# Narrow transposes and remainder products widened to the full 128x128 array, in an attention and convolution block with its gradients

## The chip, the cores and the metric

The kernel runs on one core of a Trainium2 chip. Its time is the device time of one execution in microseconds. Engines are named as in the profile: PE is TensorE (the 128x128 array), PEld its weight loads, DVE is VectorE, ACT is ScalarE, POOL is GpSimd, and SP is the sync engine, which issues nearly all DMAs here.

## The reference

One block of an E-Branchformer and its gradients, in bf16, for 2 batches of T = 4000 tokens and D = 144 channels. The results are the output and the gradients of x and of the seven weights.

```python
def _fwd_reference(x, w_qkv, w_att_out, w_mlp_in, dw_csgu, w_mlp_out, dw_merge, w_merge):
    xa = _layernorm(x)
    q, k, v = split(einsum('btd,de->bte', xa, w_qkv), 3)
    p = softmax(einsum('btd,bsd->bts', q, k) * D ** (-0.5))
    glob = einsum('btd,de->bte', einsum('bts,bsd->btd', p, v), w_att_out)
    u, g = split(gelu(einsum('btd,de->bte', xa, w_mlp_in)), 2)
    gc = depthwise_conv5(_layernorm(g), dw_csgu)          # over time, 5 taps
    loc = einsum('btd,de->bte', u * gc, w_mlp_out)
    m = concatenate([glob, loc])
    m = m + depthwise_conv5(m, dw_merge)
    return x + einsum('btc,cd->btd', m, w_merge)

_out, _vjp = jax.vjp(_f, x, w_qkv, w_att_out, w_mlp_in, dw_csgu, w_mlp_out, dw_merge, w_merge)
_grads = _vjp(grad_out)
```

(The splits and the convolutions are written out in the original; `depthwise_conv5` and `split` stand here for slices and a loop over the taps.)

## The kernel before

Tokens lie in blocks of 128 on the partitions: 32 blocks (NBK) a batch, in 8 groups (NGR) of four. A row of 144 channels doesn't fit 128 partitions once it is transposed. So every transposed tensor has a main part (channels 0 to 127) and a remainder of 16 channels (DR = 16), and much of the code deals with remainders: they are put together from several tensors (`t3`: 32 + 16 = 48 columns; `g80` and the tap arrays: 5 x 16 = 80).

`bounded` runs three stages for each batch, and one at the end.

- `phase_head` norms x, transposes it and makes the arrays Q and B that the attention needs.
- `phase_attn` goes through 32 rows of blocks (`unit`, `xfill`, `yz`), forward and backward in one pass. Products with QBr (L1768) use 16 rows of the array, four of them side by side. In between, `Steps` places pieces of the local branch (`pair`, `tapcorr`), a fixed order written out with `manual_schedule`. A pair of blocks calls `Chan.put` twice (once for the normed gate `gn`, once for its gradient `dgc`): four transposes into one PSUM tile (L1476 and L1478), two ACT copies, and a DMA that stores the remainder five times, shifted by one token each (`Taps.store`). `Taps.load` brings 80 rows back for the convolution. SP issues these DMAs in order with the transposing DMAs of P and S (L1786).
- `phase_tail` goes through 16 pairs of blocks in rounds h, two rounds to a group g. `turn` transposes Y (h = 0) and ug (h = 1) of a group, and stores their remainders as taps. `corr` adds up EF (L1944), the correlations behind some weight gradients. `turn_dx` transposes four parts of two blocks (L1954), `parts(i)`, the last of which is `t3`; `turn_dx2` copies them from PSUM to hT, and `dx_mm` multiplies hT by W.WIM (L1987). `out_mm` (L1969, L1970) makes the output of the pair four rounds earlier. In four last rounds `gr_part` (L2038) multiplies the same four parts by xaa, eight blocks a call, for further weight gradients. `prep`, on POOL, fills `t3` and `g80` of the next group.
- `finish_weights` makes the weight gradients from EF and gr.

A transpose on PE has the data as stationary operand, so the array's columns in use are the width of the slice that is transposed: 128, 16 or 48 here. A round of the tail stands in this order (cut):

```python
                if hf == 0 and g < NGR:
                    turn(g, 0); corr(g, 0); turn(g, 1); corr(g, 1)
                elif g < NGR:
                    corr(g, 2); corr(g, 3)
                if h < NPR:
                    tt = turn_dx(h)
                    turn_dx2(*tt)
                ...
                if 0 <= h - 4 < NPR:
                    out_mm(h - 4)
                ...
                if h < NPR:
                    dx_mm(h)
                if hf == 1 and g + 1 < NGR:
                    prep(g + 1)
```

W.WIM[:, 3, :] is set to zero before its first 48 rows are filled, in the kernel before as well.

Of the kernel before, what the change touches and what calls it, by code (L numbers as in the profile page):

```python
# [7 lines left out]
BF = mybir.dt.bfloat16  # L8
# [6 lines left out]
D = 144  # L15
DR = 16
# [1042 lines left out]
NBK = 32  # L1059
# [401 lines left out]
class Chan:  # L1461
# [8 lines left out]
    def put(self, p, src):  # L1470
        nc = self.k.nc
        t = self.t[p] = self.pool.tile([128, 260], BF, tag=self.name, bufs=3, name=self.name)
        r_ = self.pool.tile([128, 256], BF, tag=self.name + "s", bufs=2, name=self.name + "s")
        pm = self.ps.tile([128, 4, 128], BF, tag="f", name="pm")
        for j in range(2):
            nc.tensor.transpose(pm[:, j, :], src[:, j, 0:128], self.W.ident[:])  # L1476
        for j in range(2):
            nc.tensor.transpose(pm[0:DR, 2 + j, :], src[:, j, 128:D], self.W.ident[:])  # L1478
        nc.scalar.copy(r_[0:DR, :], pm[0:DR, 2:4, :].rearrange("p a b -> p (a b)"))
        nc.scalar.copy(t[:, 2:258], pm[:, 0:2, :].rearrange("p a b -> p (a b)"))  # L1480
        self.taps.store(r_[0:DR, :], p * 256, 256)
        if p == 0:
            nc.gpsimd.memset(t[:, 0:2], 0.0)
        else:
            u = self.t[p - 1]
            nc.gpsimd.tensor_scalar(t[:, 0:2], u[:, 256:258], 1.0, 0.0, op0=ALU.mult, op1=ALU.add)
            nc.gpsimd.tensor_scalar(u[:, 258:260], t[:, 2:4], 1.0, 0.0, op0=ALU.mult, op1=ALU.add)
        if p == NBK // 2 - 1:
            nc.gpsimd.memset(t[:, 258:260], 0.0)
# [389 lines left out]
def phase_tail(k, W, b, S):  # L1879


    nc, tc = k.nc, k.tc
    with ExitStack() as es:
        pp = es.enter_context(tc.tile_pool(name="tl_big", bufs=1))
# [8 lines left out]
        uT = main_arr(k, pp, "uT")  # L1893
        taps = [Taps(k, "y80_%d" % b), Taps(k, "u80_%d" % b)]
        dh = pp.tile([128, NBK, 2 * D], BF, name="dhr")
        t3 = pp.tile([128, NBK, 48], BF, name="t3r")
        EF = ps_e.tile([128, 4, 512], F32, tag="EF", name="EF")
        id_ = W.ident
        G, st = {}, {}
# [11 lines left out]

        def prep(g):
            r = slice(g * 4, g * 4 + 4)
            nc.gpsimd.tensor_scalar(t3[:, r, 0:32], dh[:, r, 256:2 * D], 1.0, 0.0, op0=ALU.mult, op1=ALU.add)
            nc.gpsimd.tensor_scalar(t3[:, r, 32:48], S.Zn[:, r, 128:D], 1.0, 0.0, op0=ALU.mult, op1=ALU.add)
            g80 = G["g80", g] = lx.tile([128, 4, 80], BF, tag="g80", name="g80")
            nc.gpsimd.tensor_scalar(g80[:].rearrange("p a (m r) -> p a m r", r=DR), G["gs", g][:, :, :, 128:D], 1.0, 0.0, op0=ALU.mult, op1=ALU.add)

        def turn(g, h):

            src = (S.Yn[:, g * 4:g * 4 + 4, :], G["ug", g])[h]
            pt = ps_t.tile([128, 8, 128], BF, tag="tp", name="pt")
            for j in range(4):
                nc.tensor.transpose(pt[:, j, :], src[:, j, 0:128], id_[:])
            for j in range(4):
                nc.tensor.transpose(pt[0:DR, 4 + j, :], src[:, j, 128:D], id_[:])
            nc.scalar.copy((yT, uT)[h][:, 2 + g * 512:2 + (g + 1) * 512], pt[:, 0:4, :].rearrange("p a b -> p (a b)"))
            r_ = wk.tile([128, 512], BF, tag="r16_%d" % h, name="r16")
            nc.vector.tensor_copy(r_[0:DR, :], pt[0:DR, 4:8, :].rearrange("p a b -> p (a b)"))
            taps[h].store(r_[0:DR, :], g * 512, 512)  # L1930

        def fill(g):
            for h in range(2):
# [11 lines left out]
                                     start=(i == 0 and q % 3 == 0), stop=(i == NBK - 1), skip_group_check=True)  # L1945

        def parts(i):
            return [(dh[:, i, 0:128], 128), (dh[:, i, 128:256], 128), (S.Zn[:, i, 0:128], 128), (t3[:, i, :], 48)]

        def turn_dx(p):  # L1950
            pt = ps_t.tile([128, 8, 128], BF, tag="tp", name="pt")
            for q in range(2):
                for n_, (p_, w) in enumerate(parts(2 * p + q)):
                    nc.tensor.transpose(pt[0:w, n_ * 2 + q, :], p_, id_[:])  # L1954
            hT = st["hT", p] = wk.tile([128, 8, 128], BF, tag="hT", bufs=2, name="hT")
            return pt, hT

        def turn_dx2(pt, hT):
            nc.scalar.copy(hT[:, 0:6, :], pt[:, 0:6, :])
            nc.scalar.copy(hT[0:48, 6:8, :], pt[0:48, 6:8, :])  # L1960

        def out_mm(p):
            g = p // 2
# [18 lines left out]
        def dx_mm(p):  # L1982
            hT = st.pop(("hT", p))
            po = ps_o.tile([128, 2, D], F32, tag="o", name="po")
            for q in range(2):
                for n_, (_, w) in enumerate(parts(0)):
                    nc.tensor.matmul(po[:, q, :], hT[0:w, n_ * 2 + q, :], W.WIM[0:w, n_, :], start=(n_ == 0), stop=(n_ == 3))  # L1987
            t = st["t", p] = wk.tile([128, 2, D], F32, tag="t", bufs=4, name="t")
            nc.vector.tensor_tensor(t[:], po[:], S.acc[:, 2 * p:2 * p + 2, :], op=ALU.add)
# [42 lines left out]
        def gr_part(r):  # L2032
            if r[0] == 0:
                st["gr"] = ps_e.tile([128, 4, 512], F32, tag="EF", name="gr")
            gr = st["gr"]
            for i in r:
                for n_, (p_, w) in enumerate(parts(i)):
                    nc.tensor.matmul(gr[0:w, n_ // 2, (n_ % 2) * D:(n_ % 2 + 1) * D], p_, S.xaa[:, i, :],  # L2038
                                     start=(i == 0 and n_ % 2 == 0), stop=(i == NBK - 1), skip_group_check=True)
# [11 lines left out]
        with tc.manual_schedule():  # L2051
            loads(0)
            load_x(0)
            loads(1)
            prep(0)
            for h in range(NPR + 4):
                g, hf = divmod(h, 2)
# [5 lines left out]
                if hf == 0 and g < NGR:  # L2063
                    turn(g, 0)
                    corr(g, 0)
                    turn(g, 1)
                    corr(g, 1)
                elif g < NGR:
                    corr(g, 2)
                    corr(g, 3)  # L2070
# [3 lines that stand above are left out]
# [15 lines left out]
                if hf == 1 and g + 1 < NGR:  # L2089
                    prep(g + 1)  # L2090
# [143 lines left out]
def bounded(k):  # L2234
    nc, tc = k.nc, k.tc
    with tc.tile_pool(name="n_w", bufs=1) as wp, tc.tile_pool(name="n_acc", bufs=1) as ap:
# [9 lines left out]
        for b in range(2):  # L2246
            with tc.tile_pool(name="n_res%d" % b, bufs=1) as res:
                S = W_()
                S.xaa = res.tile([128, NBK, D], BF, name="xaa")
                S.xaT = res.tile([128, NBK * 128], BF, name="xaT")  # L2250
                S.XR = res.tile([128, 4, 512], BF, name="XR")
                S.Q_t = res.tile([128, NBK, D], BF, name="Q_t")
                S.B_t = res.tile([128, NBK, D], BF, name="B_t")
                S.rstd_x = res.tile([128, NBK], F32, name="rstdx")
                S.ug_d = tc.dram_tile([128, NBK, D], BF, name="ug_d%d" % b)
                S.gn_d = tc.dram_tile([2 + NBK * 128 + 2, D], BF, name="gn_d%d" % b)
                nc.sync.dma_start(S.gn_d[0:2, :], k.zero[0:2, :])
                nc.sync.dma_start(S.gn_d[2 + NBK * 128:4 + NBK * 128, :], k.zero[0:2, :])
                S.dh_d = tc.dram_tile([128, NBK, 2 * D], BF, name="dh_d%d" % b)
                S.dug_d = tc.dram_tile([128, NBK, D], BF, name="dug_d%d" % b)  # L2260
                phase_head(k, W, b, S)
                with tc.tile_pool(name="n_att%d" % b, bufs=1) as at:
                    S.early = at
                    S.acc = at.tile([128, NBK, D], F32, name="acc2")
                    nc.gpsimd.memset(S.acc[:], 0.0)

                    S.Yn, S.Zn = S.Q_t, S.B_t
                    phase_attn(k, W, b, S)
                    phase_tail(k, W, b, S)
# [49 lines left out]
```

## Time and profile before

| | |
|---|---|
| median of 3 runs | 1528.79 us (1527.81 to 1530.97) |
| profiled execution | span 1533.1 us; no other time of it is given |
| granted PE clock, mean | 0.939 |
| PE busy | 1364.5 us, 89% of the span |
| DVE busy | 886.1 us, 58% |
| ACT busy | 820.7 us, 54% |
| POOL busy | 567.4 us, 37% |
| batch 0 | attention from about 80 to 624 us, tail to about 735 us |
| batch 1 | attention from about 800 to 1342 us, tail to about 1455 us |

In the profile, a form such as 128*48 128x144 on PE says that 128 rows and 48 columns of the array are used, then the partitions and elements of the operands. A duration on PE runs from the start of a product to its modelled end, and products overlap: what one costs is seen from the distance to the next one's start. The stretches of the span give busy time by engine; the chain of waits follows what ended last back from the end.

### The profile page before, as it was taken

The page shows a single profiled execution, that of the slowest core. Times are in us where ns is not written, and L with a number is a line of the kernel's source. Part 1 is how long each engine was busy: PE and PEld are TensorE (multiplying, and loading weights), DVE is VectorE, ACT ScalarE, POOL GpSimd, SP SyncE. Part 2 cuts the span into 40 slices and gives each one's busy share as a digit, 9 for nine tenths or more (in the row PEclk, how much of TensorE's full clock was granted, in tenths as well). Part 3 has the DMA queues.
Part 4 walks back from the last instruction along what each step waited for, and adds up shares of the span by engine and source line. Part 5 has one row for each costly group of instructions (what it writes and reads, how often), then busy time and mean ns, then how long its engine had stood idle before and what let it go on. Part 6 is the DMA issues. An engine that isn't in the chain of part 4 may idle for free. (4 is left out here: it accounts for less than half of the span.)

```text
span 1533.1 us, 40191 instructions
## 1 busy us (share of the span) xinstructions
PE 1364.5 (89%) x15366; PEld 990.8 (65%) x15366; DVE 886.1 (58%) x3021; ACT 820.7 (54%) x2473; POOL 567.4 (37%) x1049
## 2 busy tenths in 40 slices
PE   5989999999999999899779999999999999989932
PEld 3727767676776767687553767677667667868610
DVE  5545676676676666344335666676776676534332
ACT  4746656566656654343365666666656565444210
POOL 2233444444344433343232444344444442334200
PEclk9959999999999999999896999999999999999955
DMA  5348978898988799654525988998999988856320
GB/s 143 105 86 149 169 136 162 155 170 150 163 153 163 131 192 171 146 171 116 158 77 99 165 153 147 170 164 154 164 160 147 170 158 163 162 156 180 78 87 13
DMA packets 652289, 220.66 MB, mean 144 GB/s; under 512 B 589876, under 2 KB 649012, under 8 KB 652084
## 3 DMA queue, kind: packets, MB, share of 16 engines
q1 hardware_dynamic: 651220, 217.89, 73.0%
q8 instruction: 122, 2.00, 0.6%
q14 instruction: 83, 0.68, 0.2%
q10 hardware_dynamic: 864, 0.09, 0.0%
HBM read 58.00 MB, written 25.13 MB: 54 GB/s over the span
## 5 line engine op out<-in xcount | busy, mean ns | idle before, releaser
L1778 DVE SCALAR_TENSOR_TENSOR Sm<-pD,Pm 128x500 bf16<-128x500 f32 x512 | 331.2, 675 | 286.8 <-ACT Pm L1777 226.4
L1777 ACT ACTIVATE Pm<-pS 128x500 bf16<-128x500 f32 x512 | 294.9, 582 | 125.9 <-PE pS L1772 123.0
L1839 POOL TENSOR_TENSOR acc<-xs,acc 128x432 f32<-128x432 f32 x160 | 179.8, 1124 | 395.9 <-ACT xs L1838 393.9
L1834 PE MATMUL X<-Bt,Pm 128*128 128x144 bf16 x2048 | 293.6, 227 | 1.0 <-DVE Bt L1806 1.0
L1833 PE MATMUL X<-Qs,Sm 128*128 128x144 bf16 x2048 | 293.7, 227 | 0.5 <-POOL Qs L1797 0.5
L1833 PEld LDWEIGHTS <-Sm 128*128 128x128 bf16 x2048 | 201.5, 98 | 19.2 <-issue 2.6
L1834 PEld LDWEIGHTS <-Pm 128*128 128x128 bf16 x2048 | 201.2, 98 | 18.8 <-issue 2.1
L1772 PE MATMUL pS<-xaT,QTm 128*128 128x500 bf16 x512 | 162.0, 400 | 0.0
L1772 PE MATMUL pD<-xaT,BTm 128*128 128x500 bf16 x512 | 160.1, 396 | 0.0
L1838 ACT COPY xs<-X 128x432 f32<-128x432 f32 x160 | 83.2, 520 | 138.4 <-PE X L1834 137.4
L1816 PE MATMUL y<-xaa,PT 128*128 128x144 bf16 x2048 | 150.4, 227 | 1.2 <-DVE B_t L1824 1.2
L1768 PE MATMUL pD<-XR,QBr 16*128 16x500 bf16 x512 | 131.0, 392 | 21.1 <-DVE Sm L1778 19.6
L1816 PE MATMUL y<-xaa,ST 128*128 128x144 bf16 x2048 | 149.0, 226 | 0.0
L1816 PEld LDWEIGHTS <-PT 128*128 128x128 bf16 x2048 | 134.1, 98 | 9.2 <-issue 1.6
L1816 PEld LDWEIGHTS <-ST 128*128 128x128 bf16 x2048 | 131.9, 98 | 6.5
L1841 DVE TENSOR_TENSOR acc<-X,acc 128x432 f32<-128x432 f32 x192 | 111.1, 578 | 42.3 <-PE X L1834 42.3
L1768 PE MATMUL pS<-XR,QBr 16*128 16x500 bf16 x512 | 117.3, 395 | 5.4 <-ACT Pm L1777 4.1
L1777 ACT ACTIVATION_READ_ACCUMULATOR Pm<-pS 128x1 f32 x512 | 102.2, 200 | 0.0
L1772 PEld LDWEIGHTS <-QTm 128*128 128x128 bf16 x512 | 29.3, 98 | 106.6 <-issue 106.6
L1772 PEld LDWEIGHTS <-BTm 128*128 128x128 bf16 x512 | 52.4, 102 | 65.3 <-issue 11.4
L2009 POOL TENSOR_SCALAR cc<-xaa,n 128x144 f32<-128x144 bf16 x64 | 36.2, 572 | 99.3 <-DVE n L2006 84.1
L1768 PEld LDWEIGHTS <-QBr 16*128 16x128 bf16 x1024 | 30.3, 91 | 61.7 <-issue 36.7
(584 smaller groups left out, 2602.6 us busy)
## 6 DMA issues: line engine op xcount, KB each, us to landing
gs<-in_grad_out_dram SPq DMA_DIRECT2D x24, 720.0 KB
gtap<-gn_d SPq DMA_DIRECT2D x16, 720.0 KB
dh_d<-dh SPq DMA_DIRECT2D x32, 144.0 KB
dhr<-dh_d SPq DMA_DIRECT2D x16, 288.0 KB
gs<-in_grad_out_dram SPq DMA_DIRECT2D x8, 540.0 KB
xg<-in_x_dram SPq DMA_DIRECT2D x28, 144.0 KB
dug_d<-dug SPq DMA_DIRECT2D x16, 144.0 KB
gn_d<-gn_t SPq DMA_DIRECT2D x32, 72.0 KB
```

Source lines behind the costliest of these rows:

```text
L1768: nc.tensor.matmul(o_[:, 0:SC], QBr[rr, bi, :], S.XR[rr, c2, 0:SC], start=True, stop=False)
L1772: nc.tensor.matmul(p_[h][:, 0:SC], w_[:, bi, :], S.xaT[:, c0 + h * SC:c0 + (h + 1) * SC], start=False, stop=True)
L1777: nc.scalar.activation(P[:, pb, c1:c1 + SC], pS[h][:, 0:SC], ACT.Exp, accum_out=ld8[:, 0, n:n + 1])
L1778: nc.vector.scalar_tensor_tensor(Sm[:, pb, c1:c1 + SC], pD[h][:, 0:SC], 1.0, P[:, pb, c1:c1 + SC], op0=ALU.mult, op1=ALU.mult, accum_out=l ...
L1816: nc.tensor.matmul(y[:, w, :], src[:, jj, :], S.xaa[:, j, :], start=(j == 0), stop=(j == NBK - 1))
L1833: nc.tensor.matmul(X[:, jj, :], Sm[:, i % NP, j * 128:(j + 1) * 128], Qs[:, i % 4, :], start=(kk == 0), stop=False)
L1834: nc.tensor.matmul(X[:, jj, :], P[:, i % NP, j * 128:(j + 1) * 128], Bt[:, i % 4, :], start=False, stop=(kk == 1))
L1838: nc.scalar.copy(xs[:, 0:nj, :], X[:, 0:nj, :])
L1839: nc.gpsimd.tensor_tensor(a_, xs[:, 0:nj, :], a_, op=ALU.add)
L1841: nc.vector.tensor_tensor(a_, X[:, 0:nj, :], a_, op=ALU.add)
L2009: nc.gpsimd.tensor_scalar(cc[:, q, :], S.xaa[:, 2 * p + q, :], n[:, 1, q:q + 1], n[:, 0, q:q + 1], op0=ALU.mult, op1=ALU.add)
```

## The change

Five places are widened to 128 columns or rows.

- In `Chan.put` and `turn`, the remainder's transpose takes channels 16 to 143 (128 wide, overlapping the main part) in place of 128 to 143. The 16 wanted rows then lie on partitions 112 to 127, the copies from PSUM take partitions 96 to 127, and the DMAs read 112 to 127.
- `t3` is 128 columns wide; a new memset on POOL in `prep` clears columns 48 to 127 of a group. Its transposes in `turn_dx` and its products in `gr_part` are 128 wide by that.
- The product of `dx_mm` with the remainder takes 128 rows of hT and W.WIM, since it takes its width from `parts`.
- hT is copied by one ACT instruction of 128x1024 in place of 128x768 and 48x256.

The order of the instructions stays as it was on every engine; 32 ACT copies go and 16 POOL memsets come. No other wait is added.

```diff
@@ Chan.put
-            nc.tensor.transpose(pm[0:DR, 2 + j, :], src[:, j, 128:D], self.W.ident[:])
-        nc.scalar.copy(r_[0:DR, :], pm[0:DR, 2:4, :].rearrange("p a b -> p (a b)"))
+            nc.tensor.transpose(pm[:, 2 + j, :], src[:, j, DR:D], self.W.ident[:])
+        nc.scalar.copy(r_[96:128, :], pm[96:128, 2:4, :].rearrange("p a b -> p (a b)"))
         nc.scalar.copy(t[:, 2:258], pm[:, 0:2, :].rearrange("p a b -> p (a b)"))
-        self.taps.store(r_[0:DR, :], p * 256, 256)
+        self.taps.store(r_[112:128, :], p * 256, 256)
@@ phase_tail
-        t3 = pp.tile([128, NBK, 48], BF, name="t3r")
+        t3 = pp.tile([128, NBK, 128], BF, name="t3r")
@@ prep
             r = slice(g * 4, g * 4 + 4)
+            nc.gpsimd.memset(t3[:, r, 48:128], 0.0)
             nc.gpsimd.tensor_scalar(t3[:, r, 0:32], dh[:, r, 256:2 * D], 1.0, 0.0, op0=ALU.mult, op1=ALU.add)
@@ turn
-                nc.tensor.transpose(pt[0:DR, 4 + j, :], src[:, j, 128:D], id_[:])
+                nc.tensor.transpose(pt[:, 4 + j, :], src[:, j, DR:D], id_[:])
-            nc.vector.tensor_copy(r_[0:DR, :], pt[0:DR, 4:8, :].rearrange("p a b -> p (a b)"))
-            taps[h].store(r_[0:DR, :], g * 512, 512)
+            nc.vector.tensor_copy(r_[96:128, :], pt[96:128, 4:8, :].rearrange("p a b -> p (a b)"))
+            taps[h].store(r_[112:128, :], g * 512, 512)
@@ parts
-            return [(dh[:, i, 0:128], 128), (dh[:, i, 128:256], 128), (S.Zn[:, i, 0:128], 128), (t3[:, i, :], 48)]
+            return [(dh[:, i, 0:128], 128), (dh[:, i, 128:256], 128), (S.Zn[:, i, 0:128], 128), (t3[:, i, :], 128)]
@@ turn_dx2
-            nc.scalar.copy(hT[:, 0:6, :], pt[:, 0:6, :])
-            nc.scalar.copy(hT[0:48, 6:8, :], pt[0:48, 6:8, :])
+            nc.scalar.copy(hT[:], pt[:])
```

## The prediction

> **What bounds the kernel now.** I read the page's busy line first, then stretches of the span, then the chain of waits, and last the timeline of TensorE (PE) around each instruction that the change touches.
>
> ```profile
> PE 1364.5 (89%) x15366; PEld 990.8 (65%) x15366; DVE 886.1 (58%) x3021; ACT 820.7 (54%) x2473; POOL 567.4 (37%) x1049
> ```
>
> ```profile
> 110.00:624.00 514.00, 488.10 (x5833) 363.91 (x5830) 341.39 (x1068) 311.14 (x940) 215.72 (x390) 0.99 0.88 158
> 1380.00:1430.00 50.00, 50.00 (x661) 41.42 (x659) 24.19 (x93) 21.90 (x63) 23.11 (x44) 1.00 0.58 155
> ```
>
> The columns of the stretches are busy us (and count) on PE, its weight loads, DVE, ACT and POOL, then granted clock, DMA share and GB/s. The first row is the attention stage of batch 0: PE 488.1 of 514 us, nothing else above 71%, DMA at 0.88. The second is the steady part of the tail of batch 1: PE 50.00 of 50.00 us, the others under half, clock 1.00. A busy PE is no proof of a full one, so the question is what PE does inside those 50 us. In the chain of waits the end of the tail is PE alone:
>
> ```profile
> 1440.38 3.63 PE gr L2038 x32
> ```
>
> The timeline of PE over one round and a half of the steady tail gives the answer. Its columns are start, duration, line and operation, rows*columns of the array that are used, shape; what counts is the distance from one start to the next.
>
> ```profile
> 1393.18 0.98 PE L1987 MATMUL po<-w_IM,hT 128*128 128x144 bf16 x8
> 1394.09 0.24 PE L1944 MATMUL EF<-Q_t,gs 128*128 128x144 bf16 x1
> ...
> 1394.72 0.23 PE L1944 MATMUL EF<-Q_t,g 128*80 128x144 bf16 x1
> 1394.78 0.23 PE L1944 MATMUL EF<-ug,g 128*80 128x144 bf16 x1
> 1394.85 0.23 PE L1944 MATMUL EF<-Q_t,gs 128*128 128x144 bf16 x1
> ...
> 1395.60 0.28 PE L1954 MATMUL pt<-w_ident,dhr 128*128 128x128 bf16 x2
> 1395.71 0.22 PE L1954 MATMUL pt<-w_ident,B_t 128*128 128x128 bf16 x1
> 1395.86 0.24 PE L1954 MATMUL pt<-w_ident,t3r 128*48 128x128 bf16 x1
> 1396.03 0.28 PE L1954 MATMUL pt<-w_ident,dhr 128*128 128x128 bf16 x2
> ...
> 1396.30 0.24 PE L1954 MATMUL pt<-w_ident,t3r 128*48 128x128 bf16 x1
> 1396.46 0.49 PE L1969 MATMUL po<-w_G,yT 128*128 128x144 bf16 x5
> ...
> 1398.90 0.40 PE L1924 MATMUL pt<-w_ident,Q_t 128*128 128x128 bf16 x4
> 1399.23 0.39 PE L1926 MATMUL pt<-w_ident,Q_t 128*16 128x128 bf16 x4
> 1399.55 0.24 PE L1944 MATMUL EF<-Q_t,gs 128*128 128x144 bf16 x1
> ```
>
> From 1394.09 to 1395.60 there are 24 products of 144 columns in 1.51 us, 0.063 us each. The 80-wide ones among them (128*80) keep that pitch, in and out: 0.06 to 0.07. The 48-wide transpose of t3 does not: B_t at 1395.71, t3r at 1395.86 (0.15), the next dhr at 1396.03 (0.17). Nor does the 16-wide one of L1926. No idle time or releaser stands at these places, so it is no wait for another engine: PE loses about 0.1 us on the way into a narrow form and 0.1 us on the way out. A form of 80 does not pay, one of 48, or 16, does.
>
> The Trainium skill says why, in "TensorEngine Tiling (Array Packing)", Key Properties: the array can be cut into tiles of 32 or 64, and changing the tiling mode, not just the tile, drains the engine. The pitches above agree, with some 0.1 us for each change; the page gives no price.
>
> **The change part by part.** The references for full-size work, and the narrow transposes of the attention stage:
>
> ```profile
> 524.55 0.39 PE L1754 MATMUL pj<-w_ident,QB 128*128 128x128 bf16 x4
> 524.77 1.16 PE L1816 MATMUL y<-xaa,PT 128*128 128x144 bf16 x16
> ```
>
> ```profile
> 120.61 0.28 PE L1476 MATMUL pm<-w_ident,gn_t 128*128 128x128 bf16 x2
> 120.82 0.28 PE L1478 MATMUL pm<-w_ident,gn_t 128*16 128x128 bf16 x2
> 121.03 1.17 PE L1816 MATMUL y<-xaa,ST 128*128 128x144 bf16 x16
> ```
>
> Four full transposes take 0.22 us, 0.055 each.
>
> 1. The product with t3 in gr_part (L2038), 64 times. The chain's row has 32 products in 3.63 us; at full pitch they take 32 x 0.063 = 2.02. Saved 1.61 x 8 calls = 12.9 us.
> 2. The remainder product of dx_mm (L1987), 48 rows to 128, 64 times. Eight products take 1393.18 to 1394.09, 0.91 us; at full pitch 0.50. Saved 0.41 x 32 = 13.1 us.
> 3. The t3 transposes of turn_dx (L1954). Eight transposes take 1395.60 to 1396.46, 0.86 us, against 0.44. Saved 0.42 in the 24 rounds in which out_mm follows. In the first four rounds of each batch no out_mm stands there, PE waits for ACT instead, and the last exit hides in that wait: 0.30 x 8. Together 12.5 us.
> 4. The 16-wide transposes of turn (L1926): 1398.90 to 1399.55 is 0.65 us against 0.44. Saved 0.21 x 32 = 6.7 us.
>
> Those four lie on PE in the tail, where nothing else is near the end of a wait: 45.2 us, of which I take 44, since the rows are rounded to 10 ns at some 130 places.
>
> 5. The 16-wide transposes of put (L1478), 64 calls: four transposes take 0.42 us where 0.22 would do. In 34 calls a full-size product follows and both changes go, 0.20; in 30 calls the next is the 16-row product of L1768, another form anyway, so only the way in goes, 0.10. On PE 9.8 us. How much of it reaches the end, the chain tells. It passes through these transposes 11 times from 1083 us on, out of (18+14)/2 = 16 calls:
>
> ```profile
> 1105.00 0.21 PE pm L1478 x2
> ...
> 1291.04 0.21 PE pm L1478 x2
> ```
>
> ```profile
> L1478 PE MATMUL pm<-w_ident,dgc x18: 219/220/223, 1087.0 to 1293.6; 128*16 128x128 bf16 x18
> L1478 PE MATMUL pm<-w_ident,gn_t x14: 219/220/223, 1104.9 to 1272.9; 128*16 128x128 bf16 x14
> ```
>
> That is 0.69, and where it passes a shorter PE meets the next DVE or ACT release at once. The bounds are 0 and 9.8; I take 0.6, 5.9 us.
>
> 6. ACT's two copies of hT become one, 128x1024. In the first four rounds of each batch PE waits for the first copy alone:
>
> ```profile
> 1354.25 0.24 PE L1954 MATMUL pt<-w_ident,t3r 128*48 128x128 bf16 x1
> 1355.37 0.99 PE L1987 MATMUL po<-w_IM,hT 128*128 128x144 bf16 x8 [0.89 <-ACT hT L1959]
> ```
>
> ```profile
> 1354.52 0.80 ACT L1959 COPY hT<-pt 128x768 bf16<-128x768 bf16 x1 [1.02 <-PE pt L1954]
> 1355.21 0.36 ACT L1960 COPY hT<-pt 48x256 bf16<-48x256 bf16 x1
> ...
> 1400.33 0.57 ACT L1927 COPY yT<-pt 128x512 bf16<-128x512 bf16 x1
> ```
>
> 512 columns take 0.57 and 768 take 0.80, so 1024 take about 1.02: less than 0.80 + 0.36, but 0.22 later for the first product. Cost 0.22 x 8 = 1.8 us (bounds 0, if the copy were as short as 0.80, and 0.36 x 8 = 2.9). From the fifth round on, out_mm's 24 products (1.5 us) cover it: ACT starts 0.27 after the last transpose and would end at 1.29. Without that cover each round would cost 0.2.
>
> 7. POOL gets a memset of 128x4x80 at the head of prep, ahead of g80, for which PE waits in the next round (L1944, 128*80).
>
> ```profile
> 1398.39 0.46 POOL L1917 TENSOR_SCALAR g<-gs 128x320 bf16<-128x320 bf16 x1
> ```
>
> ```profile
> 1400.18 0.23 PE L1944 MATMUL EF<-Q_t,g 128*80 128x144 bf16 x1
> ```
>
> ```profile
> L1735 POOL MEMSET Pm<- x2: 338/338/339, 79.7 to 799.7; 128x288 bf16 x2
> ```
>
> ```profile
> L1739 POOL MEMSET QB<- x2: 525/525/525, 80.2 to 800.3; 128x512 bf16 x2
> ```
>
> 288 columns take 338 ns and 512 take 525, so 320 take about 0.365 us (bounds 0.338 and 0.525, the two rows). Count from 1394.09, the end of a dx_mm, since POOL's chain hangs on that (its cc follows DVE's sums of dx): g80 is there at 4.76 now, at 5.13 then. PE asks for it at 6.1 now. With an odd round of 4.81 - 0.42 - 0.41 = 3.98, a turn of 0.44 and ten products (0.63) it asks at 5.05. So the slack of 1.3 us is spent, and a stall of about 0.14 us (0.06 for the semaphore) appears once for each of 14 groups: 2.0 us, bounds 0 and, with 0.525, 0.30 x 14 = 4.2.
>
> 8. At nothing: the copies of r_ have 32 partitions in place of 16 and the same columns, and copies here go by columns; DMA reads 16 rows at partition 112 in place of 0, the same bytes in the same order, landing a round before they are read. SP's queue has the same entries. What it would cost if they landed later is rival (d). The weight loads:
>
> ```profile
> L1476 PEld LDWEIGHTS <-gn_t x64: 95/98/100, 120.5 to 1272.6; 128*128 128x128 bf16 x64
> ```
>
> ```profile
> L1478 PEld LDWEIGHTS <-gn_t x64: 85/87/89, 120.8 to 1272.8; 128*16 128x16 bf16 x64
> ```
>
> The first row is of a 128-wide load, the second of a 16-wide one (least, median and most ns). The 128-wide load has a median of 98 ns and the 16-wide one of 87: 11 ns more, beside the product before it. Exposed, 256 of them would be 2.8 us.
>
> Sum: 44 + 5.9 - 1.8 - 2.0 = 46 us. Against the profiled span of 1533.1 that is 1487; the page gives no other time for that execution, and its span is 4.3 us above the median of the runs, 1528.8. I take the 46 from the median: 1483 us.
>
> **The rivals.**
> (a) The attention stage gives nothing back, because DVE's and ACT's releases set its pace: 46 - 5.9, 1489 us. For it: DMA at 0.88, and five of the 16 calls off the chain. Against it: the other eleven, and PE busy 95%.
> (b) POOL's chain becomes the bound of the tail: with the memset at its upper bound (4.2 in place of 2.0), and with POOL's cc later by another 0.2 us in each of the 14 groups (2.8): 1488 us. For it: the slack of 1.3 us is used up. Against it: POOL's row shows 23 us busy in 50.
> (c) The padding doesn't do it: the lost 0.2 us belongs to the place (a change of line or of PSUM tile) and not to the width. Then nothing comes off and the costs of 6 and 7 stay on: 1529 to 1533. Against it: the 80-wide products change tile with no loss, and the full transposes of 524.55 run into a product of another line at 0.055.
> (d) Slower: the tap stores get slow. They read partitions 112 to 127 where they read 0 to 15, and in the attention stage SP waits at the tap load (L1458) until the store has landed, with the transposing DMAs of P and S queued behind it. The row is of SP's waits from 110 to 590 us: total, times, longest.
>
> ```profile
> SPq L1458 <- DMA dgC_d<-dgC0s: 9.5, 5, 2.9
> ```
>
> If each of the 64 stores took 1 us more, and all of that reached the end, the change would lose 64 and win 46: 1547 us. It decides from 46/64 = 0.72 us a store. For it: the wait is there, and DMA is at 0.88. Against it: bytes, rows and pieces are the same, and only 5 waits of this kind stand in those 480 us.
> (e) PE's weight loads grow in proportion to their columns, and nothing hides them. From 98 ns for 128 columns that is 98 x 112/128 = 86 ns for each of 256 loads and 98 x 80/128 = 61 for each of 128: 30 us of the 46 are lost, 1513 us. The rows speak against it: 87 ns for 16 columns, where proportion would give 12.
> The Trainium skill has this rule in "TensorE: Matmul & The Clock Gate", LDWEIGHTS (loading the stationary operand): the time is columns / 1.2 ns, whatever the rows; by its figures the loads would grow by 93 and 67 ns, an estimate of 32 us. The trace does not agree with its 13 ns for 16 columns.
>
> **How the numbers follow.** The forecast has a chance of 0.63, (a) 0.16, (b) 0.11, (c) 0.05, (d) 0.03, (e) 0.02. About 0.2% is what a measurement of this kernel can tell from no change. Faster is the forecast with (a), (b) and (e), 0.92; same is most of (c), 0.04; slower is (d) and the rest of (c), 0.04. The low end of the range is all of 45.2 + 9.8 less 2: 1476 us. The high end has (a) and the upper costs of 6 and 7 together, a gain of 36.8 us, and some 4 us off it for a clock that dips elsewhere (the page's span differs from the median by as much): 1497 us.
>
> **What would show it.** Right: the starts around t3r, L1926 and L1478 at 0.055, gr's pieces in the chain near 2.0 us for 32, dx_mm's eight at 0.50, a steady odd round at 4.0 us in place of 4.81, hT's first product in the early rounds 1.3 us after the last transpose. Wrong: pitches of 0.15 that stay (c); PE waiting for POOL's g80 by more than 0.3 us in each group (b); L1768 waiting for DVE by what put no longer takes (a); SP's wait at L1458 longer (d); loads of 180 ns (e). A granted clock that falls in one of the runs' tails would hide some us of the gain.

## The result, and the profile after

The changed kernel takes 1495.53 us, the median of 4 runs (1492.18 to 1497.14), beside 1528.93 us for the kernel before in 4 runs (1527.81 to 1530.97). The medians are 33 us apart. The ratio is 0.977, with an interval of 0.974 to 0.980, which is 31 to 39 us off. In a later pairing (both kernels timed side by side again, shown below) the medians were 42 us apart. The ratios leave out two runs far above all others, 1634.08 us of the kernel before at a granted clock of 0.807 and 3511.11 us of the version with the memset late.

The page's busy line of the kernel after, to be read beside the first line shown of before:

```profile
PE 1318.6 (88%) x15366; PEld 989.9 (66%) x15366; DVE 890.4 (60%) x3021; ACT 829.3 (56%) x2441; POOL 572.9 (38%) x1065
```

PE lost 46 us of busy time (1364.5 to 1318.6), ACT and POOL gained 8.6 and 5.5. The profiled execution took 1494.56 us with a span of 1492.7; the span before was 1533.1, so 40.4 us went. The next two rows are stretches of the kernel after, with the columns as before. First the attention stage of batch 0, then a steady part of the tail of batch 1:

```profile
110.00:624.00 514.00, 486.96 (x5808) 365.32 (x5807) 341.97 (x1069) 316.39 (x941) 215.28 (x390) 0.98 0.87 158
1350.00:1390.00 40.00, 39.58 (x636) 38.85 (x634) 24.46 (x89) 20.31 (x53) 23.11 (x45) 1.00 0.69 195
```

The attention stage is as full as it was (487.0 of 514 us, 488.1 before), at a granted clock of 0.98 in place of 0.99. In the tail PE is now idle for 0.42 of 40 us, where it was idle for nothing. The chain of waits of the kernel after says for what, and shows gr_part's share:

```profile
1380.04 1.15 POOL cc L2009 x2
1381.27 0.47 POOL t L2010
1382.00 0.36 POOL t3r L1914
1382.85 0.56 POOL g L1918
1383.46 0.32 PE EF L1945 x2
...
1407.45 2.00 PE gr L2038 x32
```

gr_part's 32 products take 2.00 us, where they took 3.63. The chain, which was PE alone there, now passes through POOL once in each group: cc, t, the new memset of t3, and g80, which PE's correlations wait for. The same on PE's timeline, in one round of the steady tail of the kernel after (start, duration, line, rows*columns):

```profile
1363.39 0.66 PE L1987 MATMUL po<-w_IM,hT 128*128 128x144 bf16 x8
1363.89 0.39 PE L1925 MATMUL pt<-w_ident,Q_t 128*128 128x128 bf16 x4
1364.12 0.39 PE L1927 MATMUL pt<-w_ident,Q_t 128*128 128x128 bf16 x4
1364.34 0.23 PE L1945 MATMUL EF<-Q_t,gs 128*128 128x144 bf16 x1
...
1364.90 0.23 PE L1945 MATMUL EF<-ug,gs 128*128 128x144 bf16 x1
1365.27 0.26 PE L1945 MATMUL EF<-Q_t,g 128*80 128x144 bf16 x1
...
1366.62 0.28 PE L1955 MATMUL pt<-w_ident,dhr 128*128 128x128 bf16 x2
1366.73 0.22 PE L1955 MATMUL pt<-w_ident,B_t 128*128 128x128 bf16 x1
1366.79 0.22 PE L1955 MATMUL pt<-w_ident,t3r 128*128 128x128 bf16 x1
1366.84 0.28 PE L1955 MATMUL pt<-w_ident,dhr 128*128 128x128 bf16 x2
...
1367.07 0.48 PE L1969 MATMUL po<-w_G,yT 128*128 128x144 bf16 x5
```

Eight products of dx_mm now take 0.50 us (1363.39 to 1363.89; 0.91 before), eight transposes of turn 0.45 (to 1364.34; 0.65), and t3r starts 0.06 after B_t with the next dhr 0.05 behind it (0.15 and 0.17); turn_dx's eight take 0.45 (1366.62 to 1367.07; 0.86). The one hole is at 1364.90: the next start is 0.37 later where 0.06 is the pitch, 0.30 us lost to POOL's g80. POOL at that place:

```profile
1363.81 0.36 POOL L1914 MEMSET t3r<- 128x320 bf16 x1
...
1364.62 0.59 POOL L1918 TENSOR_SCALAR g<-gs 128x320 bf16<-128x320 bf16 x1
```

The memset takes 0.36 us, as estimated; g80's own copy takes 0.59 here and not 0.46. It now runs beside other work than before; whether that is what slows it was not tried.

The sums by stage come from the distances between fixed instructions. In batch 1, where both kernels have the same 3.4 us at half clock, the tail from the last y to the first gr went from 93.0 us to 80.4, and the gr part from 19.3 to 12.5: 19.4. Batch 0 gave 0.8 less, since its gr part takes 13.3 us after (19.3 with narrow products at full clock, in the profile of put alone). A product of out_mm waits there for a tap load, which it doesn't in the profile of before:

```profile
713.30 0.24 PE L1970 MATMUL po<-w_G,r 80*128 80x144 bf16 x1 [0.67 <-DMA r<-y]
```

So the two tails gave 38.0 us. (Before, batch 0's gr part ends at 741 us; the table ahead of the prediction has the tail's end at 735.) A steady group (two rounds) takes 9.15 us in place of 10.93. The attention stage, from its first L1768 to its last y, got no shorter in these two profiles: 541.6 to 542.5 us in batch 0, 538.9 to 541.3 in batch 1. That is partly the clock. It falls to half for 3.4 us or multiples of that, and each us at half clock costs such a stretch 0.4 to 0.5 us: the two tails of before take 94.6 us with 6.8 of it and 93.0 with 3.4, and batch 0's attention takes 542.5 us with 49 of it here and 535.8 with 34 in the version with the memset late, whose attention is the same code. Before's attention stages had 79 us of it, after's had 93, which is some 6 us of time. One of the places, in before:

```profile
340.00:346.00 6.00, 5.77 (x65) 4.17 (x65) 5.30 (x18) 3.51 (x10) 3.78 (x6) 1.00 0.75 152
```

and in after, with clock 0.72 and 43 products of PE in place of 65:

```profile
340.00:346.00 6.00, 5.48 (x43) 3.62 (x43) 5.00 (x18) 2.55 (x8) 2.50 (x5) 0.72 0.76 153
```

Rows of the attention compared at full clock alone (28 of the 32 in a stage, the median of the profiles in which a row was undisturbed) add up to 458.15 us before and 456.27 after, 1.9 less a stage, 3.7 in all. So at equal clocks the change is worth 38.0 + 3.7 = 41.7 us; by the spans, 40.4 plus some 1.6 for 3.6 us more at half clock over both batches, it is 42.0.

### The profile page after: what moved, and what is told of

Its sections match the earlier page's. It is cut to its first block, busy times and chain, and to the rows that moved or that the text cites. A ratio compares the mean times of both kernels' runs of the same rounds, so it can differ in the third digit from the quotient of the medians.

```text
span 1492.7 us, 40175 instructions
## 1 busy us (share of the span) xinstructions
PE 1318.6 (88%) x15366; PEld 989.9 (66%) x15366; DVE 890.4 (60%) x3021; ACT 829.3 (56%) x2441; POOL 572.9 (38%) x1065
## 5 line engine op out<-in xcount | busy, mean ns | idle before, releaser
L1833 PEld LDWEIGHTS <-Sm 128*128 128x128 bf16 x2048 | 202.1, 99 | 19.3 <-issue 2.9
L1768 PE MATMUL pD<-XR,QBr 16*128 16x500 bf16 x512 | 132.6, 393 | 24.4 <-DVE Sm L1778 23.4
L1816 PEld LDWEIGHTS <-PT 128*128 128x128 bf16 x2048 | 137.1, 100 | 7.6 <-issue 2.0
L1841 DVE TENSOR_TENSOR acc<-X,acc 128x432 f32<-128x432 f32 x192 | 111.0, 578 | 41.8 <-PE X L1834 41.7
L1768 PE MATMUL pS<-XR,QBr 16*128 16x500 bf16 x512 | 118.6, 396 | 5.8 <-ACT Pm L1777 4.3
L1772 PEld LDWEIGHTS <-BTm 128*128 128x128 bf16 x512 | 52.5, 103 | 65.9 <-issue 12.5
L1768 PEld LDWEIGHTS <-QBr 16*128 16x128 bf16 x1024 | 30.5, 91 | 65.6 <-issue 40.9
```

Of the source, the lines that this page charges most:

```text
L1768: nc.tensor.matmul(o_[:, 0:SC], QBr[rr, bi, :], S.XR[rr, c2, 0:SC], start=True, stop=False)
L1772: nc.tensor.matmul(p_[h][:, 0:SC], w_[:, bi, :], S.xaT[:, c0 + h * SC:c0 + (h + 1) * SC], start=False, stop=True)
L1816: nc.tensor.matmul(y[:, w, :], src[:, jj, :], S.xaa[:, j, :], start=(j == 0), stop=(j == NBK - 1))
L1833: nc.tensor.matmul(X[:, jj, :], Sm[:, i % NP, j * 128:(j + 1) * 128], Qs[:, i % 4, :], start=(kk == 0), stop=False)
L1841: nc.vector.tensor_tensor(a_, X[:, 0:nj, :], a_, op=ALU.add)
```

## The experiments

Edits are against the kernel after, except where they say before. The first four ran together, with before at 1533.93 us (23 runs), then four with before at 1536.68 (11), then two with before at 1534.94 (9). The kernel before itself moves by some us from one pairing to the next, so ratios are compared, and only within a pairing.

There is a second comparison, since each of these runs has its granted clock on record. For the kernel before, 42 runs in the three pairings serve for it. They lie between 0.933 and 0.943, and a run is 1.3 us longer for each 0.001 less. A line fitted to all these runs, with one slope and an offset for each kernel, gives what a kernel is worth at equal clock.

**Is it the tail alone?** The kernel before with the widened transposes of put alone:

```diff
 # in the kernel before, Chan.put only
-            nc.tensor.transpose(pm[0:DR, 2 + j, :], src[:, j, 128:D], self.W.ident[:])
+            nc.tensor.transpose(pm[:, 2 + j, :], src[:, j, DR:D], self.W.ident[:])
...
-        self.taps.store(r_[0:DR, :], p * 256, 256)
+        self.taps.store(r_[112:128, :], p * 256, 256)
```

> The kernel before with the widening in put alone (L1478): the tail keeps its narrow forms. As predicted (0.6 of PE's 9.8 us reach the end): 1523 us, 6 below before. Theory that the attention stage absorbs it, because PE meets a release by ACT or DVE that comes no earlier: within 2 us of before, and the attention stages of the trace as long as before (521 and 539 us from the first L1768 to the last, in the profiles of before). Theory that the wide put makes the attention stage slower: 1531 to 1533. In all three the start-to-start distances around L1478 fall from 0.15 to 0.055.

1533.62 us in 12 runs, ratio 0.999 (0.997 to 1.001). The prediction's 5.9 us is a ratio of 0.996, outside of the interval; the 3.7 us of the rows, 0.9976, is inside. At equal clock put alone is 3.9 us faster than before, give or take 1.1, which agrees with the rows. Its complement, with put as before:

```diff
-            nc.tensor.transpose(pm[:, 2 + j, :], src[:, j, DR:D], self.W.ident[:])
+            nc.tensor.transpose(pm[0:DR, 2 + j, :], src[:, j, 128:D], self.W.ident[:])
...
-        self.taps.store(r_[112:128, :], p * 256, 256)
+        self.taps.store(r_[0:DR, :], p * 256, 256)
```

> The changed kernel with put as before: widening only in the tail (turn, t3, gr_part, dx_mm). If the tail is the whole gain: within 2 us of the changed kernel, 1495. As predicted (put brings 6): 1501. If the wide put costs: 1491 to 1493. The tail of each batch is 92 to 94 us long from the last product of y to the last of gr, as in the changed kernel (117 and 112 before).

1496.93 us, ratio 0.975 (0.972 to 0.978), 37 us off: all but a few us of the change are in the tail.

**What does POOL's memset cost?** It moves behind g80, so that g80 is as early as before:

```diff
@@ prep
-            nc.gpsimd.memset(t3[:, r, 48:128], 0.0)
...
             nc.gpsimd.tensor_scalar(g80...)
+            nc.gpsimd.memset(t3[:, r, 48:128], 0.0)
```

> The changed kernel with POOL's memset of t3 moved behind g80 in prep. Theory that the 0.365 us memset is what makes g80 late: PE's waits for g80 in the steady groups (13 of the 17 in the changed kernel) go, and the time falls by about 2 us, to 1493.5. Rival, that POOL's cc chain is late anyway: the waits stay, shorter, and the time is 1495.

1496.12 us, ratio 0.975 (0.971 to 0.978), some 39 us off: the time tells nothing at this size, the profile does. PE's idle time before the correlations in the kernel after (us, times):

```profile
  POOL g L1918: 14.6, 17
```

and with the memset late:

```profile
  POOL g L1917: 9.7, 5
```

The wait falls from 14.6 us in 17 places to 9.7 in 5, what it was before the change (9.3 in 4). Yet a group falls from 9.15 to 9.03 us only, not by 0.30 (the second group of each batch, with a longer wait, from 9.51 to 9.03). What is late next is the copies of turn: PE waits 0.21 us ahead of turn_dx for a PSUM tile that DVE's copy of r_ has to free, which waits for ACT's copy of yT, which stands behind ACT's work on the last dx. The distances between groups add up to 1.0 us less in each batch, 2.0 in all.

**Is 128 needed, and where does a form begin to be narrow?** t3 64 and 80 columns wide, with hT copied in two pieces again (shown for 80; for 64 the numbers are 64):

```diff
-        t3 = pp.tile([128, NBK, 128], BF, name="t3r")
+        t3 = pp.tile([128, NBK, 80], BF, name="t3r")
-            nc.gpsimd.memset(t3[:, r, 48:128], 0.0)
+            nc.gpsimd.memset(t3[:, r, 48:80], 0.0)
-            ... (t3[:, i, :], 128)]
+            ... (t3[:, i, :], 80)]
-            nc.scalar.copy(hT[:], pt[:])
+            nc.scalar.copy(hT[:, 0:6, :], pt[:, 0:6, :])
+            nc.scalar.copy(hT[0:80, 6:8, :], pt[0:80, 6:8, :])
```

> The changed kernel with t3 64 columns wide in place of 128 (memset of 16 columns, hT's remainder copied for 64 rows in a copy of its own as in the kernel before). Theory that what is paid is a change of the array's form, full for more than 64 rows or columns: the 0.1 us at each side of t3's transposes, of its products in gr_part and of dx_mm's remainder come back whole, and of the tail's 44 us only turn's 6 to 7 are left: 1522 to 1526. Rival, that the loss goes with the part of the array that is unused (80 of 128 columns at 48, 64 at 64): a fifth of it is won, 1515. Rival, that zero padding of any width does it: 1495.

1533.47 us, ratio 0.999 (0.997 to 1.001). The timeline of PE and a piece of the chain, with t3 64 wide:

```profile
1397.85 0.22 PE L1955 MATMUL pt<-w_ident,B_t 128*128 128x128 bf16 x1
1398.00 0.24 PE L1955 MATMUL pt<-w_ident,t3r 128*64 128x128 bf16 x1
1398.17 0.29 PE L1955 MATMUL pt<-w_ident,dhr 128*128 128x128 bf16 x2
```

```profile
1444.01 3.69 PE gr L2039 x32
```

The pitches are those of 48 columns, 0.15 and 0.17, and gr's 32 products take 3.69. dx_mm's eight products take 0.91 us with 64 rows of hT, as with 48. A form of 64 pays in full. A steady group takes 10.66 us, 0.27 under before, where turn's two calls were put at 0.42: turn's transposes save 0.39 of PE's time there, and 0.10 of it is lost again ahead of turn_dx. That this kernel, with turn and put widened, isn't faster than before by the ratio goes with its clock: its 12 runs have 0.932 to 0.937, and its profile has 109 us at half clock over both batches, before's 96. At equal clock it is 7.6 us faster, give or take 1.2. Why its clock is lower was not tried.

> The changed kernel with t3 80 columns wide in place of 128 (memset of 32 columns, hT's remainder copied for 80 rows in a copy of its own). Theory of the form (more than 64 columns or rows count as the full array): t3's transposes, its products and dx_mm's remainder keep the full pitch of 0.055 to 0.063 us; the memset is shorter by 0.2 us and hT's first copy is early again, so it is equal or 1 to 5 us faster than the changed kernel. Rival, that only 128 is full: the tail is 112 to 117 us, and the time 1530.

1489.78 us, ratio 0.969 (0.966 to 0.971). The timeline and the chain with t3 80 wide:

```profile
1397.21 0.23 PE L2039 MATMUL gr<-xaa,B_t 128*128 128x144 bf16 x1
1397.27 0.23 PE L2039 MATMUL gr<-xaa,t3r 128*80 128x144 bf16 x1
1397.34 0.29 PE L2039 MATMUL gr<-xaa,dhr 128*128 128x144 bf16 x2
```

```profile
1400.76 2.00 PE gr L2039 x32
```

Full pitch, 0.06, and 2.00 us; dx_mm's eight products take 0.51. The change of form lies between 64 and 80 columns. That is as the Trainium skill's "TensorEngine Tiling (Array Packing)" lists the configurations, in Tiling Modes: with 128 rows there are 128, 64 and 32 columns, so that 64 is a mode of its own and 80 is not. The kernel after itself, in the same pairing:

> The changed kernel unaltered, timed again beside the kernel before, as the measure for the other kernels of this call: 1495 to 1498, with 92 to 94 us of tail in each batch and ACT's second copy of put starting 389 ns after its first.

1494.43 us, ratio 0.972 (0.968 to 0.976), 42 us off. The intervals of 80 and 128 columns overlap. At equal clock the kernel after is 41 us faster than before in the first pairing and 42 in this one (39 and 40 at equal us at half clock, which are a larger share of a shorter run).

**Why does put give less than its transposes?** In the attention of the kernel after, some rows get longer by 0.1 to 0.3 us, each in all profiles with the widened put, while most get shorter by just what PE saves, 0.1 or 0.2. One of them (0.22 longer), ACT before:

```profile
234.52 0.20 ACT L1777 ACTIVATION_READ_ACCUMULATOR Pm<-pS 128x1 f32 x1
234.61 0.34 ACT L1479 COPY gnC0s<-pm 16x256 bf16<-16x256 bf16 x1
234.86 0.36 ACT L1480 COPY gnC<-pm 128x256 bf16<-128x256 bf16 x1
```

PE before:

```profile
233.91 0.27 PE L1476 MATMUL pm<-w_ident,gn_t 128*128 128x128 bf16 x2
...
235.34 0.44 PE L1504 MATMUL pc<-w_dg,dgC 128*128 128x128 bf16 x5
```

ACT after:

```profile
235.95 0.20 ACT L1777 ACTIVATION_READ_ACCUMULATOR Pm<-pS 128x1 f32 x1
236.18 0.36 ACT L1479 COPY gnC0s<-pm 32x256 bf16<-32x256 bf16 x1
236.56 0.37 ACT L1480 COPY gnC<-pm 128x256 bf16<-128x256 bf16 x1
```

PE after:

```profile
235.34 0.27 PE L1476 MATMUL pm<-w_ident,gn_t 128*128 128x128 bf16 x2
...
236.99 0.44 PE L1504 MATMUL pc<-w_dg,dgC 128*128 128x128 bf16 x5 [0.26 <-ACT gnC L1480]
```

Before, the copy of 16 partitions (L1479) starts 0.09 us after an instruction of 0.20, well before that one ends, and L1480 0.25 later. After, L1479 takes partitions 96 to 127: it starts 0.23 after the same instruction, behind its end, and L1480 another 0.38 later, behind L1479's end. In 44 of the 64 calls L1479 starts before the instruction ahead has ended, or within 0.1 us of its end. There the median distance from that end to L1479's start went from -106 to +24 ns, and from L1479's start to L1480's from 264 to 389. PE's convolution (L1504) waits for L1480: 1.43 us from L1476 before, 1.65 after, though PE's work in between is 0.2 shorter. Is it the 32 partitions, or that they start at 96? Two edits tell that. Copies over all 128 partitions, in put and in turn:

```diff
-        nc.scalar.copy(r_[96:128, :], pm[96:128, 2:4, :].rearrange("p a b -> p (a b)"))
+        nc.scalar.copy(r_[:], pm[:, 2:4, :].rearrange("p a b -> p (a b)"))
...
-            nc.vector.tensor_copy(r_[96:128, :], pt[96:128, 4:8, :].rearrange("p a b -> p (a b)"))
+            nc.vector.tensor_copy(r_[:], pt[:, 4:8, :].rearrange("p a b -> p (a b)"))
```

> The changed kernel with the copies of r_ in put (ACT) and turn (DVE) over all 128 partitions in place of 96 to 127; the stores read 112 to 127 as before. Theory that a copy which starts at partition 96 can't overlap its neighbours on its engine (in the changed kernel it starts 24 ns after the one ahead has ended, and the next one 389 ns after its start; in the kernel before -106 and 264): the overlap comes back, put's pair of copies takes 0.62 us in place of 0.76, the rows of the attention that got longer (7, 9, 20 of each batch) do not, and the time falls by 1 to 3 us. Rival, that the number of partitions or PE's earlier end sets these times: 389 and the time stay.

1491.53 us, ratio 0.970 (0.967 to 0.972), inside the kernel after's interval. And 32 partitions from 0 on in put, so that the taps get other channels than the reference's:

```diff
-        nc.scalar.copy(r_[96:128, :], pm[96:128, 2:4, :].rearrange("p a b -> p (a b)"))
+        nc.scalar.copy(r_[0:32, :], pm[0:32, 2:4, :].rearrange("p a b -> p (a b)"))
...
-        self.taps.store(r_[112:128, :], p * 256, 256)
+        self.taps.store(r_[0:DR, :], p * 256, 256)
```

> The changed kernel with put's copy of r_ taken from partitions 0 to 31 in place of 96 to 127, and the store from 0 to 15, so that the taps get channels 16 to 31 in place of 128 to 143: the same work on the wrong channels, a probe of ACT's times alone. Theory that the start partition breaks the overlap: the first copy starts about 0.1 us before the one ahead of it has ended, the second 264 ns after the first. Rival, that 32 partitions in place of 16 do it: 24 ns after, and 389.

1490.84 us in one run, beside 1534.94. The same place on ACT, first with 128 partitions:

```profile
237.09 0.20 ACT L1777 ACTIVATION_READ_ACCUMULATOR Pm<-pS 128x1 f32 x1
237.19 0.37 ACT L1479 COPY gnC0s<-pm 128x256 bf16<-128x256 bf16 x1
237.44 0.39 ACT L1480 COPY gnC<-pm 128x256 bf16<-128x256 bf16 x1
```

and with 32 from partition 0:

```profile
236.80 0.20 ACT L1777 ACTIVATION_READ_ACCUMULATOR Pm<-pS 128x1 f32 x1
236.89 0.35 ACT L1479 COPY gnC0s<-pm 32x256 bf16<-32x256 bf16 x1
237.15 0.36 ACT L1480 COPY gnC<-pm 128x256 bf16<-128x256 bf16 x1
```

Both start as early as before (0.09 and 0.10, then 0.25 and 0.26), and the medians are back at -106 to -108 and at 263. So it is where the copy starts, not how many partitions it has. (Both its input and its output start elsewhere; which of the two counts was not tried.) Of the three rows that had become longest, by 0.20, 0.22 and 0.27 us, two are now 0.02 to 0.10 shorter than before and the third is 0.09 longer. Two other rows, 0.10 longer each in the kernel after, stay so with either edit. The rows that all profiles have at full clock add up to 437.25 us with the full copies, 437.92 with those from 96, and 439.40 before. That is 0.7 us a stage, 1.3 in all, which the times can't show.

**Together.** The full copies, the late memset and hT copied as 768 and 256 columns of 128 partitions; then the same with t3 80 wide:

```diff
 # copies as above, in put and turn; memset behind g80; and
-            nc.scalar.copy(hT[:], pt[:])
+            nc.scalar.copy(hT[:, 0:6, :], pt[:, 0:6, :])
+            nc.scalar.copy(hT[:, 6:8, :], pt[:, 6:8, :])     # [0:80, 6:8] with t3 80 wide
```

> The same, with the memset of t3 behind g80, and with hT in two copies (128x768, then 128x256), so that the first product of dx_mm waits for the first alone. 5 us less of waits for g80, 0.2 us less in each of the 8 early rounds, and what the copies bring: 7 to 10 us below the changed kernel, 1486 to 1489. If the waits for g80 are only replaced by others: 1492 to 1494.

1491.76 us, ratio 0.970 (0.967 to 0.973).

> t3 80 columns wide, the copies of r_ over all partitions, the memset behind g80. The pieces that helped one by one, together: rows 7 and 9 of the attention as short as with the full copies, steady groups of 9.03 us, first copy of hT early. 1486 to 1490 where the changed kernel has 1494 to 1496. If the steady group stays at 9.03, the DVE copy of r_ that frees PSUM for turn_dx is the next thing late there.

1489.64 us, ratio 0.971 (0.969 to 0.974). The versions with t3 80 wide have the lowest medians, but neither of them stands apart from the kernel after's interval: what they take away are terms of 1 to 2 us.

## Where the prediction was right and where not

The mechanism was right: the loss sat on the change of form and not on the place, and it went where the width went. The time came out inside of the range, but near its upper end: 1495.5 us, where the sum gave 1483. Rival (c) falls by the pitches of the kernel after, and by 64 columns against 80, which differ in nothing but the width.

1 to 4. Terms summed to 45.2, taken as 44. gr_part 3.63 to 2.00, dx_mm 0.91 to 0.50, t3's transposes 0.86 to 0.45, turn 0.65 to 0.45: each as worked out. A steady group saved 2.08 us on PE (10.93 to 9.15, with 0.30 of a stall in it), as the items have it; the 1.2 taken off for rounding wasn't needed. With 6 and 7 the tail was to give 40.2, and it gave 38.0.

6. The copy of hT. One of the early rounds on PE in the kernel after, and ACT's copy in it:

```profile
1343.39 0.22 PE L1955 MATMUL pt<-w_ident,t3r 128*128 128x128 bf16 x1
1344.72 0.67 PE L1987 MATMUL po<-w_IM,hT 128*128 128x144 bf16 x8 [1.10 <-ACT hT L1960]
```

```profile
1343.65 1.01 ACT L1960 COPY hT<-pt 128x1024 bf16<-128x1024 bf16 x1 [0.53 <-PE pt L1955]
```

1.01 us for 1024 columns (1.02 estimated), and the product 1.33 us after the last transpose, where it was 1.12: 0.2 in 8 rounds, 1.6 against 1.8.

7. POOL was undersized. The stall is 0.30 us in most groups, not 0.14, and 4.2 against 2.0 over the 14. The memset's price was right, but g80's copy was carried over as 0.46 from before, where it is 0.59 in the groups that stall. Rival (b), which had it at 4.2 and cc later besides, was half true: POOL is on the chain of the tail now. But with the stall taken away only 0.12 of 0.30 comes back, as the next release is 0.18 behind it.

5. put was oversized: 5.9 taken, 3.7 by the rows. The step that failed is "where it passes a shorter PE meets the next DVE or ACT release at once", together with item 8, which had the copies of r_ at nothing because "copies here go by columns". Their durations did stay (345 to 362 ns, then 365). What the prediction didn't look at is where a copy starts relative to its neighbours: that cost ACT 0.27 us a call (0.13 ahead of the two copies and 0.14 in them), and where PE waits for L1480 the row got longer. Yet with the full copies only 1.3 of the missing 2.2 us come back. The other 0.9, and why 4 to 5 of PE's 9.8 us don't reach the end even then, stay open. Rival (a) is true in part.

8. (d) falls: SP's waits at the tap load, from 110 to 590 us, in the kernel after.

```profile
SPq L1458 <- DMA dgC_d<-dgC0s: 7.7, 4, 2.1
```

They were 9.5 us in 5 places. One load of the tail, though, which item 8 had "landing a round before they are read", now comes late: the 0.67 us of batch 0's gr part. (e) falls with the pitches: L1478's loads are 98 ns with 128 columns, and the transposes stand 0.055 apart.

The time. Predicted 46 us off and 1483; 33 off and 1495.5 in the first pairing, 42 in the second. Most of the gap between 46 and 41.7 is 2.2 of item 7, 2.2 of item 5 and 0.7 of the late load, less the 1.2 of rounding. The gap between 33 and 42 lies in the kernel before (1528.93 and 1536.68), not in the kernel after (1495.53 and 1494.43). The clock differs from run to run of one kernel (99 and 89 us at half clock in the two profiles of the kernel after), and over both batches the twelve profiles hold between 75 us (memset late) and 109 us (64 wide), some 15 us of time. On the line of the 42 runs 1529 us would need a clock of some 0.944; what the first pairing's runs of before had is not on record, so this cause is likely and not shown. The prediction allowed 4 us for the clock, at the upper end of the range, and without them the 1495.5 would have been outside: that it is inside owes something to luck. It also took the 46 off the runs' median (1528.8), while the profile that it was worked out from was a run of some 1535 us (span 1533.1, with the 1.9 around it that the kernel after shows); off that the 46 give 1489. The bound of 0.2% for what can be told from no change was too small as well: the medians of the kernel before went from 1528.93 to 1536.68 over the pairings.

## What to carry to other kernels

Look at the distances between starts where a matmul's rows or columns fall to 64 or less between full ones: here it cost 0.1 us on the way in and 0.1 on the way out, and a padding that costs nothing on PE took it away, with 80 columns as good as 128. When an edit shifts where a small copy starts, look at how it overlaps its neighbours on its engine and not only at how long it is; and when PE gets shorter, ask for each of its waits what is 0.2 us behind, since that took 0.18 of 0.30 us a group here, and 6 of put's 9.8 us did not reach the end, only 1.3 of them by the copies.

## What the runs showed of the hardware that was not expected

A copy on ACT that starts at partition 96, among instructions that start at 0, doesn't overlap with them: +24 ns after the end of the one ahead in place of -106, and 389 ns to the next start in place of 264. On DVE the same, for the copy of r_ in turn (medians of the 14 calls with an instruction right behind): the next one starts 32 ns after its end, where it started 71 ns before it, and with 128 partitions again 83 before it. The Trainium skill states this for Vector instructions, in "VectorE: DVE Perf Modes", Two Vector instructions with no wait between them: one whose operand starts in another quadrant of 32 partitions than the last one read from, or written to, the same memory is held until all earlier Vector instructions have finished. DVE's rows agree with it, and ACT's show the same.

The clock fell in four of the six gr parts that had narrow products (before, put only, 64 wide; 6.8 us in three of them and 3.4 in the fourth), and in none of the eighteen with 80 or 128 columns. At full clock a narrow gr part takes 19.3 us, with the dip 20.6 to 22.3. Whether the narrow forms bring the clock down there was not tried.
